# Three zero products fewer, the loads in one queue, and the stores of an attention and channel-mix kernel in quarters

## The chip, the cores and the metric

The kernel runs on one core of a Trainium2 chip. The metric is the time on the device of one execution, in microseconds (us); the median of several runs is compared. A profile is one further execution, taken by the hardware profiler, with a record of each instruction.

The core has four engines that compute, each with its own queue in which instructions start in order: TensorE (PE in the profile, with PEld for the loads of its weights), VectorE (DVE), ScalarE (ACT) and GpSimd (POOL). SyncE (SP) only issues transfers. A "q" behind a name (SPq, ACTq, POOLq) is the part of the engine that issues and waits. Transfers run on 16 DMA engines.

## The reference

Two layers follow each other. The first is attention with polynomial features, on 4 batches, 4 heads, 1088 positions and 32 dimensions a head:

```python
def phi(x):                                   # r = 8, so 64 features
    a = einsum('rd,bhsd->bhsr', S1, x)
    b = einsum('rd,bhsd->bhsr', S2, x)
    return einsum('bhsi,bhsj->bhsij', a, b).reshape(..., r * r)
q_p, k_p = phi(q), phi(k)
kv  = einsum('bhsf,bhsd->bhfd', k_p, v)
z   = sum(k_p, axis=2)
num = einsum('bhsf,bhfd->bhsd', q_p, kv)
den = einsum('bhsf,bhf->bhs', q_p, z)[..., None] + 1e-06
attn = num / den
```

Its output, with the heads side by side, is the x (4 x 1088 x 128) of the second layer, a channel mix with the previous position:

```python
xk = mu_k * x + (1 - mu_k) * x_prev
xr = mu_r * x + (1 - mu_r) * x_prev
k  = maximum(xk @ w_k, 0)                     # 128 -> 1024
v  = (k * k) @ w_v                            # 1024 -> 128
out = sigmoid(xr @ w_r) * v
```

## The kernel before, in words

Everything fits on the core at once. The kernel is a list of some 370 short tasks, written out by hand in the string `ORDER`; each task is a function of the kernel that puts one or a few instructions on one engine. The order in the string is the order on each engine. Nothing is moved by a planner; waits between engines come from the data. A name is followed by its batch (0 to 3) or its group of outputs (0 to 8), and by a letter for the engine where there is a choice (A for ScalarE, V for VectorE, G for GpSimd, S for SyncE); `@` gives the PSUM banks.

The loads are a list of their own, `LOADS`, issued in this order ahead of all tasks: `k01@S` is the second half of k of batch 0, issued by SyncE, `s0` and `s1` are S1 and S2, `v00` to `v03` the quarters of v of batch 0, `w0` to `w2` the weights. The two rows of mu (lines 168 and 169) are issued after the list. The framework hands out eight semaphores in turn to the transfers that SyncE and ScalarE issue, loads and stores alike, in the order in which the program puts them; a transfer waits until the one eight places ahead of it has landed. GpSimd's transfers have eight others.

The tasks around the change, for batch b:

- `kturn.b.y` (L262): VectorE transposes half y of k, as soon as it is loaded. `qturn.b` (L344) does the same for q.
- `smk`, `smz` (L209, L201): TensorE spreads S1 and S2; `sevk` (L213) and `sevz` (L204) put them into SK and ZL on VectorE, `sqc` (L216) copies SK four times on GpSimd.
- `kproj.b.j` (L273): projections of k. Form P has tiles of 32 columns, four beside each other; form W has 64 columns, two beside each other. `abev.b.j` (L248) copies them out on ScalarE.
- `zmm.b` (L300), `zev.b`, `wmm.b` (L308), `wsq.b` (L312): the sum z, its copy, its row product on TensorE, and its place in SQ on VectorE.
- `abw.b.g` (L353, L367): projections of q against SQ, which give the row for the denominator too; `abwev`, `pw`, `dred` (L393), `drec` (L398) and `an` turn it into 1/den and the scaled factor, on ScalarE, GpSimd and VectorE.
- `kp` and `kvmm` (L321): features of k, and kv. `mumm` (L220) turns the rows of mu.
- `zz.n@bank` (L188): n products of zeros, 512 columns each, that nothing reads. There are 18 in the kernel, all in the first 17 us.
- `f1`, `relu`, `sq`, `f2`, `rr`, `sig`, `fin` (L581): the channel mix for a group of 512 output rows (256 in group 8). From about 27 us on TensorE does mostly this.
- `st.g.S` (L595): store of group g, 128 partitions by 512 numbers, 256 KB. Its target is written as 4 x 32 rows of 512. `st.g.t.S` stores quarter t of it, 32 partitions. In the kernel before, groups 0, 1, 3, 2, 6 and 7 (in this order) are stored whole by SyncE, and the last three groups, 5, 4 and 8, in quarters by three engines.

Of the kernel before, what the change touches and what calls it, by code (L numbers as in the profile page):

```python
# [71 lines left out]
def kernel(  # L72
# [53 lines left out]

    def load(what):
# [12 lines left out]
        elif x == "w":  # L140
            if b == 0:
                e.dma_start(wk_f[:], moe_w_k)
            elif b == 1:
                e.dma_start(wr_f[:], moe_w_r)
            else:
                e.dma_start(wv_f[:], moe_w_v.rearrange("(c p) d -> p c d", p=P))
        else:
            y, z = int(name[2]) // 2, int(name[2]) % 2
            m = 9 - z
            s = v[b].rearrange("h (a y t) d -> y a h t d", y=2, t=17)[y, :, :, 9 * z:9 * z + m, :]  # L150
            e.dma_start(vin[b][64 * y + z:64 * y + 64:2, :, :m, :].rearrange("p h m d -> p h (m d)"),
                        s.rearrange("a h m d -> a h (m d)"))

# [493 lines left out]
```

## Time and profile before

| what | value |
|---|---|
| median of 3 runs | 83.06 us (82.38 to 83.06) |
| the profiled execution's own time | 82.54 us |
| its span, from first to last instruction | 80.7 us |
| TensorE busy | 74.1 us, 92% of the span |
| VectorE busy | 65.4 us, 81% |
| ScalarE busy | 56.0 us, 69% |
| GpSimd busy | 47.4 us, 59% |
| read from and written to HBM | 7.80 MB and 2.23 MB |

The time of an execution is the span and what lies around it, 1.84 us here. A busy TensorE also counts products that wait in the pipeline. The chain of waits is the work that ended last, followed back from the last instruction: its steps are what the time is made of, the busy shares are not.

### The profile page before, as it was taken

What the parts mean: (1) busy time and instruction counts of PE and PEld (TensorE: products, weight loads), DVE (VectorE), ACT (ScalarE), POOL (GpSimd) and SP (SyncE); (2) the same over time, 40 slices, a digit from 0 to 9 for tenths busy, and PEclk for the clock granted to TensorE, in tenths of its full rate; (3) what the DMA queues carried; (4) which work ended last, traced back from release to release, by engine and by line L of the source; (5) the groups of instructions that cost most, each with busy time, mean ns of one, the idle gap of its engine ahead of it and who ended that gap; (6) DMA issues with size and microseconds to landing.
All of it is one profiled execution on the core that took longest, in us unless ns stands there. A gap on an engine that the chain in (4) does not pass through costs nothing.

```text
span 80.7 us, 3273 instructions
## 1 busy us (share of the span) xinstructions
PE 74.1 (92%) x1410; PEld 52.2 (65%) x1410; DVE 65.4 (81%) x102; ACT 56.0 (69%) x88; POOL 47.4 (59%) x68
## 2 busy tenths in 40 slices
PE   4999999989999899999999999999999999999600
PEld 1376378847809458576876785778666876899500
DVE  4563820899967999999999999899989999999500
ACT  0703106116547799899899999999979988999400
POOL 6245960786999997589506499209901718702720
PEclk9999999999999999999999999999999999999995
DMA  1999999999999600000000012220022220112570
GB/s 20 312 349 307 292 337 362 231 263 310 382 299 245 181 9 0 8 0 12 0 0 12 0 15 71 83 86 24 0 27 96 55 89 0 15 51 109 176 238 5
DMA packets 7258, 10.24 MB, mean 127 GB/s; under 512 B 762, under 2 KB 4060, under 8 KB 7244
## 3 DMA queue, kind: packets, MB, share of 16 engines
q1 hardware_dynamic: 6840, 9.46, 40.2%
q10 hardware_dynamic: 308, 0.41, 1.5%
q8 instruction: 11, 0.18, 0.9%
q0 software_dynamic: 96, 0.16, 0.8%
q14 instruction: 3, 0.02, 0.1%
HBM read 7.80 MB, written 2.23 MB: 124 GB/s over the span
## 4 chain that ended last, share of the span: by engine, by line
PE 61%; POOL 12%; DVE 10%; ACT 6%; issue 4%; POOLq 1%; ACTq 0%
PE ps L526 13%; PE ps L558 12%; PE ps L188 8%; PE ps L433 6%; PE ps L367 6%; POOL kp L255 5%; PE ps L273 5%; ACT k L534 5%; PE ps L321 3%; DVE k L536 3%; PE ps L571 3%; DVE osb L581 2%; DVE XK L505 2%; DVE k L255 2%; POOL pw L255 1%
## 5 line engine op out<-in xcount | busy, mean ns | idle before, releaser
L534 ACT ACTIVATE k<-ps 128x1024 bf16<-128x1024 f32 (+1 forms) x32 | 29.7, 976 | 1.1 <-DVE XK L505 0.3
L558 PEld LDWEIGHTS <-k 128*128 128x128 bf16 x272 | 16.9, 98 | 4.2 <-issue 0.5
L526 PE MATMUL ps<-XK,wk 128*128 128x512 bf16 (+1 forms) x72 | 19.2, 367 | 0.2 <-DVE XK L464 0.2
L558 PE MATMUL ps<-wv,k 128*128 128x128 bf16 x272 | 19.1, 219 | 0.0
L255 POOL TENSOR_TENSOR kp<-ab 128x1280 f32<-128x1280 f32 (+1 forms) x8 | 17.3, 2178 | 1.0 <-ACT ab L248 1.0
L255 POOL TENSOR_TENSOR k<-k 128x1024 bf16<-128x1024 bf16 (+1 forms) x6 | 10.5, 1751 | 11.8 <-DVE k L255 9.2
L255 DVE TENSOR_TENSOR k<-k 128x1024 bf16<-128x1024 bf16 (+1 forms) x21 | 14.1, 708 | 0.3 <-PE ps L558 0.3
L255 DVE TENSOR_TENSOR qp<-an,ps 128x1152 f32<-128x1152 f32 (+1 forms) x8 | 10.1, 1269 | 0.0
L546 ACT ACTIVATE k<-k 128x1024 bf16<-128x1024 bf16 (+1 forms) x9 | 9.1, 1028 | 0.4 <-PE ps L558 0.3
L188 PE MATMUL ps<-zero 128*128 128x512 bf16 x18 | 7.7, 560 | 1.2 <-DVE warm L155 1.2
L262 DVE STREAM_TRANSPOSE kT<-k 128x576 f32<-128x576 f32 x8 | 5.9, 753 | 3.1 <-DMA k<-in_k_dram 3.1
L526 PEld LDWEIGHTS <-wk 128*128 128x128 bf16 x72 | 6.1, 98 | 3.3 <-issue 0.7
L255 POOL TENSOR_TENSOR pw<-abw 128x272 f32<-128x272 f32 (+2 forms) x5 | 3.3, 650 | 7.6 <-ACT abw L248 7.6
L420 DVE STREAM_TRANSPOSE qf<-qp 128x2176 f32<-128x2176 f32 x3 | 7.3, 2435 | 0.0
L248 ACT COPY ab<-ps 128x256 f32<-128x256 f32 (+1 forms) x7 | 2.7, 396 | 6.1 <-PE ps L273 5.9
L367 PE MATMUL ps<-SQ,qT 128*64 128x96 f32 (+1 forms) x144 | 6.6, 250 | 0.0
L581 DVE TENSOR_TENSOR osb<-ps,r 128x512 f32<-128x512 f32 (+1 forms) x9 | 5.8, 648 | 0.9 <-ACT r L576 0.5
L273 PEld LDWEIGHTS ps<-SK,kT 128*32 128x32 f32 (+1 forms) x200 | 5.3, 145 | 1.4 <-issue 0.8
L273 PE MATMUL ps<-SK,kT 128*32 128x64 f32 (+1 forms) x200 | 6.1, 256 | 0.0
L248 ACT COPY X<-ps 128x512 f32<-128x512 f32 (+2 forms) x12 | 4.9, 434 | 1.8 <-PE ps L485 1.2
L367 PEld LDWEIGHTS ps<-SQ,qT 128*64 128x64 f32 (+1 forms) x144 | 5.5, 131 | 0.5 <-DVE SQ L312 0.3
L321 PE MATMUL ps<-kp,v 128*32 128x64 f32 x288 | 5.7, 222 | 0.0
(88 smaller groups left out, 102.4 us busy)
## 6 DMA issues: line engine op xcount, KB each, us to landing
k<-in_k_dram SPq DMA_DIRECT2D x7, 272.0 KB, 6.5
q<-in_q_dram SPq DMA_DIRECT2D x3, 544.0 KB
out_dram<-osb SPq DMA_DIRECT2D x6, 256.0 KB
v<-in_v_dram SPq DMA_DIRECT2D x8, 144.0 KB, 4.5
v<-in_v_dram SPq DMA_DIRECT2D x8, 128.0 KB, 5.2
q<-in_q_dram SPq DMA_DIRECT2D x2, 272.0 KB
...
```

The costliest lines, as they stand in the source:

```text
L188: nc.tensor.matmul(PS[:, banks[0], :], zero[:, :P], zero[:], skip_group_check=True)
L248: nc.scalar.copy(o, i)
L255: (nc.vector if eng == "V" else nc.gpsimd).tensor_mul(o, a, b)
L273: nc.tensor.matmul(_ap(d, [[n, 2], [1, 32]]), sb["kT", b][:, m, w * c:w * c + w], SK[:, :, :H].rearrange("p x h r -> p x (h r)"), skip_gro ...
L321: nc.tensor.matmul(o[32 * h:32 * h + 32, :F], vin[b][:, h, m, :], sb["kp", b, j][:, 4 * (m - KG[j][0]) + h].rearrange("p i j -> p (i j)"), ...
L367: nc.tensor.matmul(o[32 * w * c:32 * w * c + 32 * w, n:n + 96], sb["qT", b][:, u:u + w, :].rearrange("p u a -> p (u a)"), SQ[b][:, x:x + H ...
L420: nc.vector.transpose(sb["qf", b][:, s0:s1].rearrange("p s f a -> p (s f a)"), sb["qp", b][:, s0:s1].rearrange("p s i j -> p (s i j)"))
L526: nc.tensor.matmul(h[:, c, :], wk[:, P * (2 * cp + c):P * (2 * cp + c) + P], x, skip_group_check=True)
L534: nc.scalar.activation(o, h, RELU)
L546: nc.scalar.activation(o, i, SQUARE)
L558: nc.tensor.matmul(o[:, i * P:i * P + P], k2[:, i * P:i * P + P], wv[:, 2 * cp + c, :], start=(cp == 0 and c == 0 and i == 0), stop=(cp == ...
L581: nc.vector.tensor_mul(o[:].rearrange("p i f -> p (i f)")[:, :n], ps["o", g][:, :n], sb["r", g][:, :n])
```

## The change

- In `LOADS`, k01 goes from ScalarE's queue to SyncE's, so that all loads but S1 are issued by SyncE in one row. The two rows of mu are issued by GpSimd, behind its first memsets and ahead of the list of loads, in place of ScalarE.
- `zz.4@2` ahead of `zmm.0` becomes `zz.1@2`.
- The tile of zeros is 128 x 128 in place of 128 x 512; the product reads the same 128 columns four times.
- Groups 0, 1, 3, 2, 6 and 7 are stored in quarters, all by SyncE, at the same place in the order.
- Branches on `SPREAD` come in for another layout of k and v; `SPREAD` is empty, so they do nothing.

The lines of `ORDER` behind the first store are broken differently in the diff; their order is the same.

```diff
+SPREAD = {}
 LOADS = """
-s0@A k00@S k01@A s1@S q00@S q01@S k10@S k11@S v00@S v02@S v01@S v03@S q1@S w0@S w1@S k20@S k21@S v10@S v12@S v11@S
+s0@A k00@S k01@S s1@S q00@S q01@S k10@S k11@S v00@S v02@S v01@S v03@S q1@S w0@S w1@S k20@S k21@S v10@S v12@S v11@S
...
 ORDER = """
-kp.0.0.G kturn.1.0 abev.0.1.A zz.4@2 zmm.0@0 kturn.1.1 zev.0.A zz.3@2 wmm.0 qturn.0 kproj.1.1.W@1 kproj.1.0.W@2
+kp.0.0.G kturn.1.0 abev.0.1.A zz.1@2 zmm.0@0 kturn.1.1 zev.0.A zz.3@2 wmm.0 qturn.0 kproj.1.1.W@1 kproj.1.0.W@2
...
-f1.3.1@56 f2.0.3 relu.3.1.A f2.1.1 dred.2.2.V f1.3.2@01 fin.0 st.0.S sq.3.0.A f1.2.1@56 drec.2.2 relu.3.2.V f2.1.2
+f1.3.1@56 f2.0.3 relu.3.1.A f2.1.1 dred.2.2.V f1.3.2@01 fin.0 st.0.0.S st.0.1.S st.0.2.S st.0.3.S sq.3.0.A f1.2.1@56
...
-f2.7.3 f1.5.3@67 fin.6 st.6.S sq.5.2.A f1.4.2@45 relu.5.3.V f1.4.1@12 xb.2.G relu.4.2.A f2.5.0@0 f2.5.1 fin.7 st.7.S
+f2.7.3 f1.5.3@67 fin.6 st.6.0.S st.6.1.S st.6.2.S st.6.3.S sq.5.2.A f1.4.2@45 relu.5.3.V f1.4.1@12 xb.2.G relu.4.2.A
+f2.5.0@0 f2.5.1 fin.7 st.7.0.S st.7.1.S st.7.2.S st.7.3.S relu.4.1.A f1.4.3@67 sq.5.3.V f1.8.0@45 f2.5.2 sq.4.0.V
...
-    zero = const.tile([P, 512], BF16)
+    zero = const.tile([P, P], BF16)
...
+    nc.gpsimd.dma_start(mu_row[:1, :], moe_mu_k.rearrange("(x d) -> x d", x=1))
+    nc.gpsimd.dma_start(mu_row[1:, :], moe_mu_r.rearrange("(x d) -> x d", x=1))
     for what in LOADS.split():
         load(what)
-    nc.scalar.dma_start(mu_row[:1, :], moe_mu_k.rearrange("(x d) -> x d", x=1))
-    nc.scalar.dma_start(mu_row[1:, :], moe_mu_r.rearrange("(x d) -> x d", x=1))
...
-            nc.tensor.matmul(PS[:, banks[0], :], zero[:, :P], zero[:], skip_group_check=True)
+            nc.tensor.matmul(PS[:, banks[0], :], zero[:], _ap(zero[:], [[0, 4], [1, P]]), skip_group_check=True)
```

## Rows read from the trace of the kernel before

**Rows 1.** The page: busy tenths of the span in 40 equal slices.
```profile
PE   4999999989999899999999999999999999999600
...
DMA  1999999999999600000000012220022220112570
```

**Rows 2.** The chain of waits in order of time: start us, us, what.
```profile
5.26 2.10 PE ps L273 x72
7.36 1.82 PE ps L188 x4
...
10.97 1.20 PE ps L273 x36
...
35.30 0.56 PE ps L273 x40
```

**Rows 3.** Timeline, 3 to 14 us, by engine: start us, us, engine, line, operation [idle before].
```profile
3.58 1.44 DVE L262 STREAM_TRANSPOSE kT<-k 128x576 f32<-128x576 f32 x2 [0.78 <-DMA k<-in_k_dram]
...
5.22 0.89 POOL L216 COPY SQ<-SK 128x96 f32<-128x96 f32 x4 [2.79 <-DVE SK L213]
...
7.43 0.37 ACT L248 COPY ab<-ps 128x256 f32<-128x256 f32 x1 [0.43 <-PE ps L273]
...
8.43 0.78 DVE L262 STREAM_TRANSPOSE kT<-k 128x576 f32<-128x576 f32 x1 [0.38 <-DMA k<-in_k_dram]
9.13 1.27 DVE L344 STREAM_TRANSPOSE qT<-q 128x1088 f32<-128x1088 f32 x1
...
11.01 0.21 DVE L312 TENSOR_TENSOR SQ<-ps,m 128x48 f32<-128x48 f32 x1 [0.61 <-PE ps L308]
...
13.94 0.49 POOL L255 TENSOR_TENSOR pw<-abw 128x144 f32<-128x144 f32 x1 [2.55 <-ACT abw L248]
```

**Rows 4.** Timeline of TensorE: zero products (L188), wide projections of k (L273) and of q (L367).
```profile
9.57 1.24 PE L188 MATMUL ps<-zero 128*128 128x512 bf16 x3
...
12.57 0.85 PE L367 MATMUL ps<-SQ,qT 128*64 128x96 f32 x16
...
16.41 0.82 PE L188 MATMUL ps<-zero 128*128 128x512 bf16 x3
...
25.53 1.27 PE L273 MATMUL ps<-SK,kT 128*64 128x64 f32 x36
```

**Rows 5.** Timeline of SyncE and VectorE, 20 to 24 us.
```profile
20.54 0.60 SPq L151 DMA_DIRECT2D v<-in_v_dram  x1
...
21.24 1.27 DVE L344 STREAM_TRANSPOSE qT<-q 128x1088 f32<-128x1088 f32 x1
...
23.20 0.47 DVE L393 TENSOR_REDUCE den<-pw 128x34 f32<-128x306 f32 x1 [0.69 <-POOL pw L255]
```

**Rows 6.** Stretches: length, busy us of PE, PEld, DVE, ACT, POOL, PEclk, DMA share, GB/s.
```profile
1.75:3.00 1.25, 1.25 (x5) 0.43 (x3) 1.01 (x4) 0.61 (x1) 0.68 (x8) 1.00 0.91 250
3.00:4.30 1.30, 1.30 (x12) 0.43 (x11) 0.72 (x2) 0.88 (x2) 0.00 (x0) 1.00 0.96 345
...
74.00:75.25 1.25, 1.25 (x24) 1.08 (x21) 0.73 (x2) 1.25 (x4) 1.12 (x2) 1.00 0.26 102
```

**Rows 7.** Groups by line, GpSimd from 60 us: busy us, mean ns of one, idle before.
```profile
L595 POOL DMA_DIRECT2D out_dram<-osb x3 | 1.7, 559 | 0.6 <-DVE osb L581 0.6
```

**Rows 8.** Waits of SyncE's queue, 44 us to the end: us in total, times, longest.
```profile
SPq L595 <- DVE osb L581: 24.7, 6, 7.5
...
SPq L642 <- DMA out_dram<-osb: 1.5, 1, 1.5
SPq L595 <- DMA out_dram<-osb: 0.8, 1, 0.8
```

**Rows 9.** Timeline of the tail: ScalarE's queue, SyncE's queue.
```profile
77.00 0.43 ACTq L595 DMA_DIRECT2D out_dram<-osb  x1
...
77.20 0.79 SPq L595 DMA_DIRECT2D out_dram<-osb  x2
```

**Rows 10.** DMA issues from 75.8 us: count, KB each, median us to landing.
```profile
out_dram<-osb POOLq DMA_DIRECT2D x1, 32.0 KB, 2.1
```

More of the change, by code (lines that the diff above doesn't have):

```diff
@@ L49 @@
 f1.3.0@56 abwev.2.1.A qf.3.2 f2.0.2 relu.3.0.A pw.2.2.G^sq.1.3.V f1.2.0@01 f2.1.0@2 xb.1.G^sq.1.3.V relu.2.0.A
-f1.3.1@56 f2.0.3 relu.3.1.A f2.1.1 dred.2.2.V f1.3.2@01 fin.0 st.0.S sq.3.0.A f1.2.1@56 drec.2.2 relu.3.2.V f2.1.2
-an.2.2.G relu.2.1.A f2.1.3 kp.2.1.G kvmm.2.0@7 qp.2.0 sq.3.2.A xmm.3@0156 sq.2.0.A fin.1 st.1.S sq.3.1.G qp.2.1
-kvmm.2.1 xev.3.0.A f1.3.3@23 xev.3.1.A xtev.3.V f2.3.0@4 kvev.2.V relu.3.3.A xs.3 f1.2.2@56 xk.3.2 f1.2.3@01
-relu.2.2.A f2.3.1 rr.3@2 sq.2.1.V relu.2.3.A kdmm.2 f1.6.0@56 sq.2.2.V f2.3.2 relu.6.0.A sq.3.3.V f1.6.1@01 qf.2.2
@@ L54 @@
-f2.2.0@3 sq.2.3.G^sq.3.3.V sig.3 f2.3.3 relu.6.1.A f1.7.0@56 f2.2.1 relu.7.0.A rr.2@2 xb.3.G f1.6.2@01 fin.3 st.3.S
-kvcp.2.A f2.2.2 relu.6.2.A xmm.2@4567 sq.6.0.V sig.2 sq.7.0.V sq.6.1.V f2.2.3 xev.2.0.A f2.6.0@2 sq.6.2.V xtev.2.A
-f1.7.1@01 xev.2.1.A fin.2 st.2.S xs.2^sq.6.2.V f2.6.1 relu.7.1.A xk.2.2 f1.7.2@67 rr.6@3 relu.7.2.A f1.6.3@45 sq.7.1.V
+f1.3.1@56 f2.0.3 relu.3.1.A f2.1.1 dred.2.2.V f1.3.2@01 fin.0 st.0.0.S st.0.1.S st.0.2.S st.0.3.S sq.3.0.A f1.2.1@56
+drec.2.2 relu.3.2.V f2.1.2 an.2.2.G relu.2.1.A f2.1.3 kp.2.1.G kvmm.2.0@7 qp.2.0 sq.3.2.A xmm.3@0156 sq.2.0.A fin.1
@@ new lines @@
+st.1.0.S st.1.1.S st.1.2.S st.1.3.S sq.3.1.G qp.2.1 kvmm.2.1 xev.3.0.A f1.3.3@23 xev.3.1.A xtev.3.V f2.3.0@4 kvev.2.V
+relu.3.3.A xs.3 f1.2.2@56 xk.3.2 f1.2.3@01 relu.2.2.A f2.3.1 rr.3@2 sq.2.1.V relu.2.3.A kdmm.2 f1.6.0@56 sq.2.2.V
+f2.3.2 relu.6.0.A sq.3.3.V f1.6.1@01 qf.2.2 f2.2.0@3 sq.2.3.G^sq.3.3.V sig.3 f2.3.3 relu.6.1.A f1.7.0@56 f2.2.1
+relu.7.0.A rr.2@2 xb.3.G f1.6.2@01 fin.3 st.3.0.S st.3.1.S st.3.2.S st.3.3.S kvcp.2.A f2.2.2 relu.6.2.A xmm.2@4567
+sq.6.0.V sig.2 sq.7.0.V sq.6.1.V f2.2.3 xev.2.0.A f2.6.0@2 sq.6.2.V xtev.2.A f1.7.1@01 xev.2.1.A fin.2 st.2.0.S
@@ L57 @@
+st.2.1.S st.2.2.S st.2.3.S xs.2^sq.6.2.V f2.6.1 relu.7.1.A xk.2.2 f1.7.2@67 rr.6@3 relu.7.2.A f1.6.3@45 sq.7.1.V
 f1.7.3@01 sig.6 f2.6.2 sq.7.2.G^sq.7.1.V relu.7.3.V relu.6.3.A f1.5.0@67 f2.7.0@3 f2.7.1 relu.5.0.A f1.5.1@01 sq.6.3.V
 f1.5.2@45 relu.5.1.A rr.7@6 sq.7.3.V f2.6.3 sq.5.0.V sig.7 f1.4.0@01 relu.5.2.V f2.7.2 sq.5.1.G^sq.5.0.V relu.4.0.A
-f2.7.3 f1.5.3@67 fin.6 st.6.S sq.5.2.A f1.4.2@45 relu.5.3.V f1.4.1@12 xb.2.G relu.4.2.A f2.5.0@0 f2.5.1 fin.7 st.7.S
-relu.4.1.A f1.4.3@67 sq.5.3.V f1.8.0@45 f2.5.2 sq.4.0.V relu.8.0.A f1.8.2@12 f2.5.3 relu.4.3.A sq.4.1.V rr.5@3
@@ L61 @@
-sq.4.2.V rr.8@4 relu.8.2.A f2.4.0@5 sq.8.0.V f1.8.1@67 sig.5 sq.4.3.V f2.4.1 relu.8.1.A f1.8.3@12 sq.8.2.V rr.4@3
-fin.5 st.5.0.S st.5.1.S st.5.2.S relu.8.3.A sq.8.1.G^sq.8.2.V f2.4.2 sig.4 f2.4.3 sq.8.3.A f2.8.0@0 fin.4 st.4.0.S
-st.4.3.S f2.8.1 sig.8 f2.8.2 f2.8.3 fin.8 st.8.2.S st.5.3.G st.4.1.A st.4.2.G st.8.0.A st.8.1.G st.8.3.A
+f2.7.3 f1.5.3@67 fin.6 st.6.0.S st.6.1.S st.6.2.S st.6.3.S sq.5.2.A f1.4.2@45 relu.5.3.V f1.4.1@12 xb.2.G relu.4.2.A
+f2.5.0@0 f2.5.1 fin.7 st.7.0.S st.7.1.S st.7.2.S st.7.3.S relu.4.1.A f1.4.3@67 sq.5.3.V f1.8.0@45 f2.5.2 sq.4.0.V
@@ L64 @@
+relu.8.0.A f1.8.2@12 f2.5.3 relu.4.3.A sq.4.1.V rr.5@3 sq.4.2.V rr.8@4 relu.8.2.A f2.4.0@5 sq.8.0.V f1.8.1@67 sig.5
+sq.4.3.V f2.4.1 relu.8.1.A f1.8.3@12 sq.8.2.V rr.4@3 fin.5 st.5.0.S st.5.1.S st.5.2.S relu.8.3.A sq.8.1.G^sq.8.2.V
+f2.4.2 sig.4 f2.4.3 sq.8.3.A f2.8.0@0 fin.4 st.4.0.S st.4.3.S f2.8.1 sig.8 f2.8.2 f2.8.3 fin.8 st.8.2.S st.5.3.G
+st.4.1.A st.4.2.G st.8.0.A st.8.1.G st.8.3.A
 """
@@ L147, in load @@
         else:
[L148 to L152, printed above, removed]
+            if b in SPREAD:
+                z = int(name[2])
+                m = 9 - z
+                s = v[b].rearrange("h (x t) d -> x h t d", t=17)[:, :, 9 * z:9 * z + m, :]
+                p = slice(z, P, 2)
+            else:
+                y, z = int(name[2]) // 2, int(name[2]) % 2
+                m = 9 - z
+                s = v[b].rearrange("h (a y t) d -> y a h t d", y=2, t=17)[y, :, :, 9 * z:9 * z + m, :]
+                p = slice(64 * y + z, 64 * y + 64, 2)
+            e.dma_start(vin[b][p, :, :m, :].rearrange("p h m d -> p h (m d)"), s.rearrange("x h m d -> x h (m d)"))
     nc.vector.memset(zero[:], 0.0)
@@ L261, in kturn @@
             sb["kT", b] = work.tile([P, 9, P], F32, name="kT", tag="kT", bufs=2)
-        nc.vector.transpose(_ap(sb["kT", b][:, 0, 64 * y:], [[1, 2], [P, 9], [2, 32]]),
+        c, n = (2 * y, 4) if b in SPREAD else (64 * y, 2)
+        nc.vector.transpose(_ap(sb["kT", b][:, 0, c:], [[1, 2], [P, 9], [n, 32]]),
                             kin[b][:, y].rearrange("p (z m d) -> p z m d", z=2, m=9))
```

## The prediction

> **What bounds the kernel now.** Read the slices of the page first [rows 1]. TensorE is nine tenths busy from the second slice to about 76 us; the DMA engines are full up to about 28 us and nearly idle after it. So the end is set by a full TensorE in the long middle, and the two places where time can be taken out are ahead of that stretch (to 26 us) and behind it (the last stores). Of the change, the zero products and the loads lie ahead of it, the stores reach behind it.
>
> Next comes the chain of waits, in order of time [rows 2]. It runs through TensorE from 1.2 to 14 us, and part of what it runs through is not work: the zero products zz.4, 1.82 us from 7.36 to 9.18. Whether they cover a wait is read from the engines around it [rows 3]. The z product zmm.0, which follows it, needs ACT's copy of the last k projection, and that copy ends at 7.43 + 0.37 = 7.80 us. From 7.8 to 9.18 the zero products stand in front of work that is ready.
>
> Last, how fast TensorE runs there [rows 4]. Three zero products take 1.24 us at 9.57 and 0.82 us at 16.41; in the chain the 72 narrow projections at 5.26 take 2.10 us (29 ns each), the 40 of the same shape at 35.30 take 0.56 us (14 ns each) [rows 2]. The first is 512 columns at 1.2 GHz, the second the pace of 2.4 GHz. The 36 wide projections of batch 1 take 1.20 us at 10.97 [rows 2], as long as the same ones at 25.53 [rows 4]: the clock has risen by 10.97, and not before the last of the three zero products began at about 10.4. I take 10.5. (The column of the granted clock reads 1.00 from the first stretches on [rows 6]; for these first microseconds the paces are the better witness.)
>
> **The three zero products: -0.9 us.** One product of the block is left: 1.82 / 4 = 0.45 us, so it ends at 7.36 + 0.45 = 7.81, when the copy is there too (7.80). zmm.0 starts at about 7.87 in place of 9.18, 1.3 us sooner, and what follows on TensorE in order (zz.3, the row product of z, kproj.1.1) moves with it: kproj.1.1 from 10.97 to 9.67. Now the next late things. kproj.1.1 needs the second k transpose of batch 1, which waits for its load and ends at 8.43 + 0.78 = 9.21 [rows 3]: 0.46 us to spare. abw.0.0 needs SQ, and VectorE makes it behind the q transpose, which ends at 9.13 + 1.27 = 10.40: ready at 10.40 + 0.21 = 10.61, while TensorE comes to it at 11 us or later. GpSimd had been idle for 2.55 us when it began pw.0.0 at 13.94 [rows 3], so it follows a shift of up to that much. Then the clock: at 9.67 it has not yet risen. From 9.67 to 10.5 the projections go at half pace, and half of 0.83 us, 0.4, is lost. 1.3 - 0.4 = 0.9 us.
>
> Bounds. If the clock rises much earlier in an execution (say by 9 us), a removed product is worth not 0.42 but 0.22 us, and the transpose at 9.21 stops the shift: about 0.4. If it rises behind 11, both kernels run the projections slow and the whole 1.3 is kept. 0.4 to 1.3, and I take the profiled execution's 0.9.
>
> Does the shift last to 28 us, from where TensorE is full? Behind 14 us the chain goes through GpSimd and VectorE, which follow each other and move as one; only the loads stand still. The tightest I find is q of batch 2 [rows 5]. Each load waits for the one eight places ahead of it in the program, so the v load at 20.54 says that this q was in by then; its transpose starts at 21.24, and 0.9 earlier is 20.34. At worst 0.2 us is missed there, and VectorE idles 0.69 us just behind, ahead of the den sum at 23.20, which takes that up. Nothing is charged.
>
> **The loads: 0.** Second half of k of batch 0: it now stands behind the first in SyncE's queue. The two are 544 KB, the engines move 250 GB/s from 1.75 to 3.00 us and 345 GB/s after [rows 6]; that is 557 thousand bytes: 312 by 3.00 and the other 245 in 0.71 us more, so at 3.7 us. Its transpose can't start before the first one, of 0.72 us, has ended: the two run back to back from 3.58 for 1.44 us [rows 3]. 0.5 us of cover. S2 (1 KB) comes in behind them, and its products stand at 3.9 us under the same two transposes. All later loads gain one issue of about 0.4 us ahead of them on SyncE, but the DMA engines are full (shares 0.91 and 0.96), and what is queued sooner does not land sooner. The two loads of mu leave the round of eight, so the first v loads wait for older ones; same answer. I take 0, between -0.2 (k00 no longer shares the engines with k01) and +0.2 (S2 later than the transposes). The mu rows cost GpSimd two issues at 0.56 us [rows 7], from about 2.4 to 3.6, inside the 2.79 us in which it waits for SK [rows 3]; without that cover 1.1 us would fall on the SQ copies. Zero rows of 128 columns in place of 512 shorten the first memset by at most 0.2 us, ahead of the same transposes: 0.
>
> **The stores: -0.4 us.** Until the last ones they are off the path: 18 more issues at about 0.4 us each are 7 us on a SyncE that waits 24.7 us for results [rows 8]. In the tail they are not. While the whole store of group 7 drains, from 74.00 to 75.25, the engines are 0.26 busy and move 102 GB/s [rows 6]: the work of four of sixteen. SyncE's quarter st.4.3 is eight places behind that store, waits 0.8 us for it [rows 8], and is issued at 77.20 with st.8.2 behind it; both issues end at 77.99 [rows 9], and 1.5 us later the program's last wait is over (79.5). In quarters, group 7 is written long before. SyncE then issues st.4.3 at 76.4 and st.8.2 at 76.8 and is done 0.8 us sooner. Next late is ACT's third store, issued at 77.00: with the 2.1 us to landing of GpSimd's 32 KB store [rows 10] it comes in at 79.1. 79.5 - 79.1 = 0.4 us. Bounds: 0, if the full engines set the last landing, to 0.7, if ACT's and GpSimd's last stores land sooner too when the engines hold nothing of group 7.
>
> The Trainium skill, "DMA: Bandwidth & Descriptors", section "Why a DMA increments its semaphore by 16 and not by 1", says that a transfer uses the largest number of engines up to 16 that divides the slowest dimension of both sides. The whole store's is 4 and the quarter's 32; the trace's 0.26 agrees with 4 of 16. Its section "Rules for kernel authors" speaks against quarters: under 64 KB one pays mostly overhead, so gather transfers; by that rule the tail would gain nothing and the sum would be 81.6 instead of 81.2.
>
> **Sum.** -0.9 + 0 - 0.4 = -1.3 us on the profiled execution, 82.54 us (its span of 80.7 and 1.84 around it): 81.24. The median of the three runs is 83.06, half a microsecond above it (one run is 82.38); from there it would be 81.76. I put the forecast between, at 81.5.
>
> **Rivals.** (a) *The clock rises later.* The zero products are also what TensorE did before the clock rose. With three fewer the rise may come later, and fp32 work goes at half pace. If it comes only behind abw.0.1: kproj.1 takes another 1.2 us, the next zero product 0.2, and the 16 products each of abw.0.0 (0.85 us at 12.57 [rows 4]) and abw.0.1 another 0.85, together 3.1; less the 1.3 saved that is 1.8 us; with the tail 82.54 + 1.8 - 0.4 = 83.9, slower. It decides from where kproj.1 runs wholly slow (rise behind 12 us, +1.2 against -1.3); behind about 13 us the tail's gain is gone as well. Against it: TensorE has no new hole, since zmm.0 is ready at once and the projections at 9.67, so the same stretch stays filled, with projections for zero products. For it: the clock had not risen by 9.57, after the 2.10 us of projections at 5.26. 13%. The Trainium skill, "TensorE: Matmul & The Clock Gate", section "What's actually happening", states that "the default state is throttled, and activity releases the throttle"; the trace agrees in that the first ten microseconds run at 1.2 GHz. By that rule the time is this rival's 83.9 if the stretch, with fewer zero products in it, no longer releases the throttle in time.
>
> (b) *The gain is taken up by the loads.* The order of loads is unchanged in bytes; if q of batch 2 or k of batch 3 lands later by a microsecond, VectorE waits there and the middle's 0.9 is gone: 82.54 - 0.4 = 82.1, or 82.6 from the median, no change. Against it the spare times above. 17%.
>
> (c) *The tail keeps its length,* since the engines or the other two issuers set it: 82.54 - 0.9 = 81.6, or 82.1 from the median. 15%.
>
> **How the numbers follow.** Forecast 55% (81.0 to 82.0), (c) 15%, (b) 17%, (a) 13%. A difference of under 1%, 0.8 us, is about what a measurement of this kernel can't tell from none. Faster by more than that: the forecast and most of (c), 68%; within: (b) and the rest, 19%; slower: (a), 13%. The range leaves out (a) and a little at the low end, where 1.3 and 0.7 would both come in: 80.8 to 82.8.
>
> **What would show it.** Right: zmm.0 at about 7.9, kproj.1.1 at about 9.7 and its 36 products between 1.2 and 1.9 us long, pw.0.0 near 13.0; the den sum of batch 1 at 22.3; stores with DMA shares well over 0.26 in short bursts; SyncE's last issue ended by 77.2 less the shift; the landing after it 79.1 less 0.9. Wrong: kproj.1 of 2.4 us and later zero products still 0.42 us apart (a); a wait of VectorE on q or k between 18 and 25 us (b); the last wait on a store ending no sooner than 79.5 less the middle's gain (c); a transpose at 3.6 that starts later, or SQ copies behind mu's issues.

## The result and the profile after

The changed kernel is slower: median 83.55 us of 20 runs (82.48 to 85.42) against 82.37 us of 20 runs of the kernel before on the same chips (81.47 to 84.75), ratio 1.0136 with a 95% interval of 1.0100 to 1.0171. The forecast was 81.5 us. The profiled execution took 83.49 us, span 81.7 us (before 82.54 and 80.7): its rows can be laid beside those of before, and they account for the 0.95 us between these two executions. Ratios here and below compare only the runs within 1.5% of the fastest run of their own kernel, medians all runs; the more runs a kernel has, the lower its fastest, so where 6 or 12 runs stand against 17 to 36 of before the two can differ by over one per cent (after_k_first: 10 of 12 runs against 3 of 23).

TensorE is nearly as full as before and the DMA engines are full as long [rows 1]; the page's slices differ little, and where the time went is not to be seen in them:

```profile
PE   5889979989999899999999999999999999999400
...
DMA  1889999999999600000000051300132200540660
```

**To 14 us.** Timeline of the changed kernel (line numbers are 12 or 13 higher than before: L188 is L200, L262 is L275, L273 is L286, L255 is L267), to be laid beside [rows 3]:

```profile
4.41 0.30 PE L221 MATMUL ps<-ident,S 16*32 16x16 f32 x8 [0.67 <-DMA S<-in_S_dram]
...
7.82 0.61 PE L200 MATMUL ps<-zero 128*128 128x512 bf16 x1
7.95 0.37 ACT L260 COPY ab<-ps 128x256 f32<-128x256 f32 x1 [0.43 <-PE ps L286]
8.36 0.53 PE L313 MATMUL ps<-ab 128*32 128x32 f32 x18
8.82 1.31 PE L200 MATMUL ps<-zero 128*128 128x512 bf16 x3
...
9.00 0.78 DVE L275 STREAM_TRANSPOSE kT<-k 128x576 f32<-128x576 f32 x1 [3.40 <-DMA k<-in_k_dram]
...
10.14 0.78 DVE L275 STREAM_TRANSPOSE kT<-k 128x576 f32<-128x576 f32 x1 [0.37 <-DMA k<-in_k_dram]
...
10.85 1.27 DVE L357 STREAM_TRANSPOSE qT<-q 128x1088 f32<-128x1088 f32 x1
10.98 1.26 PE L286 MATMUL ps<-SK,kT 128*64 128x64 f32 x34 [0.44 <-DVE kT L275]
...
14.01 0.49 POOL L267 TENSOR_TENSOR pw<-abw 128x144 f32<-128x144 f32 x1 [2.09 <-ACT abw L260]
```

TensorE waits 0.67 us for S2, the copy of the last k projection is 0.52 us later than before (7.95 for 7.43), the one zero product covers it, and zmm.0 does start sooner (8.36; 9.11 in the timeline of before). But both k transposes of batch 1 wait for their load, 3.40 and 0.37 us, and come 1.7 us later (9.00 and 10.14 for 7.26 and 8.43). TensorE then stands idle for 0.44 us, which it never did here before, and pw.0.0 is at 14.01 in place of 13.94: nothing gained in this pair of executions. The chain of waits (start us, us, what) says it most shortly; where before it ran through projections and zero products [rows 2], it now runs through a load:

```profile
3.42 6.70 DMA k<-in_k_dram
10.14 0.79 DVE kT L275
10.98 1.26 PE ps L286 x34
```

**At 51 us.** From 14 us on VectorE, ScalarE and GpSimd keep the distance of 0.07 us up to one copy of GpSimd. Timeline of the kernel before, and of the changed one:

```profile
50.71 0.23 DVE L250 COPY X<-ps 64x64 f32<-64x64 f32 x1 [0.22 <-ACT X L248]
...
51.07 0.21 POOL L498 COPY X<-X 128x31 f32<-128x31 f32 x1 [0.26 <-DVE X L250]
51.31 1.35 DVE L505 SCALAR_TENSOR_TENSOR XK<-X,rat 128x1088 bf16<-128x1088 f32 x1
```

```profile
50.78 0.23 DVE L262 COPY X<-ps 64x64 f32<-64x64 f32 x1 [0.21 <-ACT X L260]
...
51.50 0.21 POOL L511 COPY X<-X 128x31 f32<-128x31 f32 x1 [0.61 <-DVE kvs L262]
...
51.75 1.35 DVE L518 SCALAR_TENSOR_TENSOR XK<-X,rat 128x1088 bf16<-128x1088 f32 x1 [0.28 <-POOL X L511]
```

VectorE's copy, the input, ends at 50.94 and 51.01. GpSimd follows 0.13 us later before and 0.49 us later after, with nothing else to do; VectorE now waits for it, and the distance is 0.44 us from here to the last product of osb.

**The tail.** That last product (VectorE, group 8) in both kernels, before first:

```profile
76.16 0.42 DVE L581 TENSOR_TENSOR osb<-ps,r 128x256 f32<-128x256 f32 x1 [0.37 <-PE ps L558]
```

```profile
76.60 0.42 DVE L594 TENSOR_TENSOR osb<-ps,r 128x256 f32<-128x256 f32 x1 [0.37 <-PE ps L571]
...
76.83 1.10 SPq L608 DMA_DIRECT2D out_dram<-osb  x2
```

From its start to the end of the span are 80.7 - 76.16 = 4.5 us before and 81.7 - 76.60 = 5.1 us after. SyncE's last issue ends at 77.93, 1.33 us behind that start in place of 1.83 [rows 9], as forecast in sign. Yet its last wait, and GpSimd's last store, are longer than in [rows 8, 10] (waits: us in total, times, longest; DMA issues from 75.4 us: count, KB each, median us to landing):

```profile
SPq L655 <- DMA out_dram<-osb: 2.1, 1, 2.1
```

```profile
out_dram<-osb SPq DMA_DIRECT2D x4, 64.0 KB, 2.2
out_dram<-osb POOLq DMA_DIRECT2D x2, 64.0 KB, 2.5
...
out_dram<-osb POOLq DMA_DIRECT2D x1, 32.0 KB, 2.5
```

The wait ends at 77.93 + 2.1 = 80.0, and the span 1.7 us later; before it ended at 77.99 + 1.5 = 79.5, and the span 1.2 us later. So of the half microsecond some 0.1 lies ahead of the end of that wait and 0.45 behind it. The data themselves are not later: the last packet of a store ends 2.6 us behind the start of that product, before 2.7. Behind it the DMA engines move nothing in either kernel, but for one transfer of 8 KB of a queue of instructions in the changed kernel, at 81.1 us (stretches as in [rows 6], before and after; last, from the DMA queues of the changed kernel behind 75.4 us: packets, MB, share):

```profile
78.50:79.00 0.50, 0.00 (x0) 0.00 (x0) 0.00 (x0) 0.00 (x0) 0.00 (x0) 0.73 0.34 107
79.00:79.50 0.50, 0.00 (x0) 0.00 (x0) 0.00 (x0) 0.00 (x0) 0.00 (x0) 0.50 0.00 0
```

```profile
79.00:79.50 0.50, 0.00 (x0) 0.00 (x0) 0.00 (x0) 0.00 (x0) 0.00 (x0) 1.00 0.24 70
79.50:80.00 0.50, 0.00 (x0) 0.00 (x0) 0.00 (x0) 0.00 (x0) 0.00 (x0) 1.00 0.00 0
...
q14 instruction: 1, 0.01, 0.2%
```

Spans are given to 0.1 us only; the executions' own times, 0.95 us apart, leave 0.95 - 0.44 = 0.51 us for the tail. In all: 0.07 + 0.37 + 0.51 = 0.95 us.

### The profile page after: what moved, and what is told of

Read it like the earlier page. It is cut to its first block, busy times and chain, and to the rows that moved or that the text cites. A ratio compares the mean times of both kernels' runs of the same rounds, so it can differ in the third digit from the quotient of the medians.

```text
span 81.7 us, 3292 instructions
## 1 busy us (share of the span) xinstructions
PE 73.4 (90%) x1407; PEld 52.1 (64%) x1407; DVE 65.3 (80%) x102; ACT 56.1 (69%) x88; POOL 48.4 (59%) x70
## 4 chain that ended last, share of the span: by engine, by line
PE 59%; POOL 12%; DMA 8%; DVE 6%; issue 4%; SPq 3%; ACT 2%; POOLq 1%; DVEq 0%; ACTq 0%
PE ps L539 17%; PE ps L571 17%; DMA k<-in_k_dram 8%; PE ps L446 6%; PE ps L380 5%; POOL kp L267 5%; PE ps L584 4%; PE ps L334 3%; PE ps L286 2%; DVE XK L518 2%; DVE osb L594 2%; SPq L142 2%; POOL pw L267 1%; ACT k L547 1%; POOL wk L246 1%
## 5 line engine op out<-in xcount | busy, mean ns | idle before, releaser
L267 POOL TENSOR_TENSOR kp<-ab 128x1280 f32<-128x1280 f32 (+1 forms) x8 | 17.3, 2176 | 1.5 <-ACT ab L260 1.5
L267 POOL TENSOR_TENSOR k<-k 128x1024 bf16<-128x1024 bf16 (+1 forms) x6 | 10.5, 1751 | 11.8 <-DVE k L267 9.2
L267 DVE TENSOR_TENSOR k<-k 128x1024 bf16<-128x1024 bf16 (+1 forms) x21 | 14.1, 711 | 0.3 <-PE ps L571 0.3
L267 DVE TENSOR_TENSOR qp<-an,ps 128x1152 f32<-128x1152 f32 (+1 forms) x8 | 10.1, 1270 | 0.0
L275 DVE STREAM_TRANSPOSE kT<-k 128x576 f32<-128x576 f32 x8 | 5.8, 751 | 4.5 <-DMA k<-in_k_dram 4.5
L267 POOL TENSOR_TENSOR pw<-abw 128x272 f32<-128x272 f32 (+2 forms) x5 | 3.2, 649 | 7.1 <-ACT abw L260 7.1
L200 PE MATMUL ps<-zero 128*128 128x512 bf16 x15 | 6.5, 550 | 1.0 <-DVE warm L167 1.0
L286 PE MATMUL ps<-SK,kT 128*32 128x64 f32 (+1 forms) x200 | 6.4, 256 | 0.4 <-DVE kT L275 0.4
L286 PEld LDWEIGHTS ps<-SK,kT 128*32 128x32 f32 (+1 forms) x200 | 5.5, 145 | 2.0 <-issue 0.8
```

The lines of the kernel that those rows point to most:

```text
L200: nc.tensor.matmul(PS[:, banks[0], :], zero[:], _ap(zero[:], [[0, 4], [1, P]]), skip_group_check=True)
L267: (nc.vector if eng == "V" else nc.gpsimd).tensor_mul(o, a, b)
L286: nc.tensor.matmul(_ap(d, [[n, 2], [1, 32]]), sb["kT", b][:, m, w * c:w * c + w], SK[:, :, :H].rearrange("p x h r -> p x (h r)"), skip_gro ...
```

## The experiments

All kernels in one table. Those named after_..., undo_quarters, mu_none and memsets_dve are built on the changed kernel, the others on the kernel before. Columns: ratio to the kernel before; medians of this kernel and of before, measured beside it (one run: the profiled one alone); from the profiled execution the start of the second k transpose of batch 1, the start of pw.0.0, the distance from VectorE's copy to GpSimd's copy at 51 us, and the tail, from the start of the last product of osb to the end of the span (us).

| kernel | ratio (95%) | medians | k | pw.0.0 | copy | tail |
|---|---|---|---|---|---|---|
| before | | | 8.43 | 13.94 | 0.13 | 4.5 |
| changed | 1.0136 (1.0100 to 1.0171) | 83.55, 82.37 | 10.14 | 14.01 | 0.49 | 5.1 |
| only_mu | 1.0003 (0.9941 to 1.0065) | 82.90, 83.16 | 9.16 | 13.69 | 0.5 | 4.6 |
| only_k01 | 1.0008 (0.9935 to 1.0082) | 82.95, 83.16 | 9.80 | 13.67 | 0.13 | 4.6 |
| only_zz | 0.9984 (0.9931 to 1.0037) | 82.94, 83.16 | 7.86 | 14.38 | 0.13 | 4.5 |
| only_quarters | 1.0113 (1.0062 to 1.0164) | 83.31, 83.16 | 9.27 | 13.40 | 0.13 | 5.3 |
| late_quarters | 1.0001 (0.9949 to 1.0053) | 82.57, 82.62 | 8.11 | 14.69 | 0.13 | 4.8 |
| early_quarters | 1.0087 (1.0027 to 1.0147) | 82.97, 82.62 | 8.30 | 13.36 | 0.13 | 4.6 |
| undo_quarters | 1.0101 (1.0055 to 1.0147) | 83.04, 82.62 | 10.04 | 13.91 | 0.5 | 4.6 |
| mu_none | one run | 83.82, 82.62 | 10.36 | 14.22 | 0.13 | 5.3 |
| loads_only | 1.0151 (1.0047 to 1.0255) | 83.41, 82.61 | 10.58 | 14.45 | 0.5 | 4.6 |
| zz_quarters | none | 83.79, 82.61 | 8.70 | 14.64 | 0.13 | 5.1 |
| k_first | 1.0048 (0.9989 to 1.0107) | 82.84, 82.61 | 6.86 | 13.11 | 0.13 | 4.8 |
| quarters_7 | one run | 83.92, 82.61 | 9.08 | 15.27 | 0.13 | 4.4 |
| after_k_first | 1.0168 (1.0087 to 1.0249) | 83.03, 82.98 | 6.74 | 12.61 | 0.5 | 5.1 |
| after_67_whole | 1.0145 (1.0005 to 1.0285) | 83.43, 82.98 | 9.36 | 13.23 | 0.5 | 5.1 |
| after_both | 1.0061 (0.9999 to 1.0122) | 82.81, 82.98 | 8.35 | 14.04 | 0.5 | 5.2 |
| loads_k_first | 1.0120 (1.0037 to 1.0203) | 83.11, 82.98 | 8.26 | 13.90 | 0.5 | 4.6 |
| memsets_dve | one run | 85.41, 83.92 | 10.55 | 15.75 | 0.13 | 5.3 |
| k_first_one_row | none | 82.91, 83.92 | 7.10 | 13.62 | 0.13 | 4.5 |

The column of pw.0.0 also holds when TensorE's clock rose in that one execution (zero products at 0.42 us or at 0.2 us each): a pw.0.0 is read together with the k beside it. It also holds whether the second half of batch 0's k was late. In six of the nine kernels with k01 on ScalarE's queue VectorE waits 0.36 to 2.14 us for that half and transposes it at 4.73 to 6.47 us; in the other three, and in all eleven with k01 on SyncE's, the two halves run back to back.

With that scatter, single profiles are weak, and the twenty together say more. With the loads in the old order, pw.0.0 lies between 13.36 and 15.27 us in the eight kernels with k01 on ScalarE's queue and between 13.23 and 15.75 in the seven with it on SyncE's; the mean is 14.2 in both. So the stretch to 14 us came out even, and the +0.07 above is one pair out of this scatter. From pw.0.0 to VectorE's copy are 36.76 or 36.77 us in twelve kernels and 36.99 to 40.36 in the other eight. From that copy to the last product of osb are 25.45 or 25.46 us in the twelve kernels without the stop at 51 us and 25.81 to 25.83 in the eight with it: the stop costs its 0.37 us each time. With the tail's half microsecond, which all six kernels with six groups in quarters have at least, that is 0.9 of the 1.1 us that the runs show.

**Each part alone: only_mu, only_k01, only_zz, only_quarters.**

```diff
 only_mu (the same for moe_mu_r; both now ahead of the list of loads)
-    nc.scalar.dma_start(mu_row[:1, :], moe_mu_k.rearrange("(x d) -> x d", x=1))
+    nc.gpsimd.dma_start(mu_row[:1, :], moe_mu_k.rearrange("(x d) -> x d", x=1))
 only_k01
-s0@A k00@S k01@A s1@S
+s0@A k00@S k01@S s1@S
 only_zz
-zz.4@2 zmm.0@0
+zz.1@2 zmm.0@0
 only_quarters (for g = 0, 1, 3, 2, 6, 7)
-st.g.S
+st.g.0.S st.g.1.S st.g.2.S st.g.3.S
```

> The kernel before with one part of the change: the two rows of mu issued by GpSimd. Theory M (GpSimd's two transfers hold up the DMA engines): the two transposes of batch 1's k start at about 8.9 and 10.1 us, as in the changed kernel, not at 7.26 and 8.43; time at most 0.3 us longer, since the four zero products before the z product still cover most of that. Theory Q (the single queue and S2 behind k01 do it): the transposes stay at 7.3 and 8.4 within 0.2 us, time unchanged.

> The kernel before with one part of the change: the second half of batch 0's k in SyncE's queue. Theory M: the transposes of batch 1's k stay at 7.3 and 8.4 us within 0.3; the products of S start at 4.4 instead of 3.9 us, since S2 lands behind k01, and with four zero products kept all that follows moves by 0.5 us: time +0.5. Theory Q: the transposes of batch 1's k start at 8.9 and 10.1 us.

> The kernel before with one part of the change: one zero product in place of four ahead of zmm.0. Theories M and Q: zmm.0 at 7.9 us, the wide projections of batch 1 at 9.7 and not behind 11.0, pw.0.0 near 13.1, time -0.8 us, since the loads land as before. If the clock rises later for want of zero products (the prediction's first rival), the projections take over 2 us and the time is unchanged or longer.

> The kernel before with one part of the change: all stores in quarters. By the prediction -0.4 us, the last landing 3.0 us behind the start of the last product of results and not 3.4. Rival, from the changed kernel's tail (3.6): no gain, 0 to +0.2 us, and a GpSimd or ACT instruction near 51 us that starts 0.3 to 0.4 us later than its inputs allow.

Alone, neither move of a load and not the zero products can be told from no change (I had 0.8 us for the products); the quarters cost 1.1% by the ratio, 0.14 us by the medians. In these profiles k of batch 1 is later with each load edit: by 1.37 us with k01 on SyncE, by 0.73 with mu on GpSimd. The first stands out of the scatter: the seven kernels that load as before have k at 7.86 to 9.27 us, the seven with k01 on SyncE's queue in the old order at 9.36 to 10.58. The second, 9.16, does not. In only_k01 k has become the limit although all four zero products are there (timeline):

```profile
9.80 0.78 DVE L262 STREAM_TRANSPOSE kT<-k 128x576 f32<-128x576 f32 x1 [0.53 <-DMA k<-in_k_dram]
...
13.67 0.49 POOL L255 TENSOR_TENSOR pw<-abw 128x144 f32<-128x144 f32 x1 [1.52 <-ACT abw L248]
```

13.67 - 9.80 = 3.87 us from the start of the transpose to pw.0.0. In the changed kernel it is 14.01 - 10.14 = 3.87, the same to the hundredth; before it was 5.51. In only_zz k of batch 1 was not late, but the second half of batch 0's was (5.03 us; the two halves ran back to back from 3.58 before), and TensorE's clock stayed low longer in its execution, which is my rival (a) seen once:

```profile
5.03 0.78 DVE L262 STREAM_TRANSPOSE kT<-k 128x576 f32<-128x576 f32 x1 [0.61 <-DMA k<-in_k_dram]
...
9.08 1.46 PE L188 MATMUL ps<-zero 128*128 128x512 bf16 x3
...
10.77 1.84 PE L273 MATMUL ps<-SK,kT 128*64 128x64 f32 x36
...
14.38 0.49 POOL L255 TENSOR_TENSOR pw<-abw 128x144 f32<-128x144 f32 x1 [2.19 <-ACT abw L248]
```

The 36 wide projections began 0.13 us sooner than before, took 1.84 us in place of 1.27, and pw.0.0 came 0.44 us later. Counted from the transpose of that half, pw.0.0 comes 8.6 to 9.9 us later in the six kernels with four zero products, k01 on ScalarE's queue and the old order, and 8.0 to 8.3 in k_first, zz_quarters and after_k_first, with one zero product and k of batch 1 not the limit (9.35 in only_zz): by the means the products are worth some 0.8 to 1.1 us there, near the forecast's 0.9.

**Which quarters: late_quarters (groups 6 and 7), early_quarters (0, 1, 3, 2), quarters_7 (7 alone).** Edits as in only_quarters, for these groups alone.

> Kernel before with groups 6 and 7 alone in quarters (six more issues on SyncE), the four earlier stores whole. Theory T (the last stores land later because the stores ahead of them are in quarters: about 0.35 us): the whole loss of the tail is here already, 0.3 to 0.5 us, ratio about 1.005. Theory C (the cost goes with the count of SyncE's instructions: 18 more of them bring a gap of 0.45 us in its last semaphore instructions, behind the last landing): no such gap with six more, last landing to the end of the span as before (1.2 us); ratio 1.000 if C is all of it. My prediction before the result, that quarters of group 7 free SyncE's last stores: 0.4 us faster, 0.995.

> Kernel before with groups 0, 1, 3 and 2 in quarters (twelve more issues on SyncE), groups 6 and 7 whole. Theory T: the tail is that of before, 1.000. Theory C: the gap of 0.45 us ahead of the end comes with the twelve, 1.005. Third theory E (the early stores compete with work of the middle, where nothing in the profile shows it): 1.005 or more without the gap, with TensorE's work later between 45 and 75 us.

> Kernel before with group 7 alone in quarters: the very step of my forecast of the tail. Forecast: SyncE's last issue 0.4 us or more sooner behind the last product of osb, and the end of the span with it (4.2 us in place of 4.6 from the start of that product). Theory T: issue sooner, last landing later all the same, end at 4.8.

The tail by the profiles: 4.4 us with group 7 alone (a gain of 0.1, my forecast's sign, a third of its size; I had 4.2), 4.8 with 6 and 7, 4.6 with the early four, 5.1 to 5.3 in every kernel with all six (changed, only_quarters, mu_none, zz_quarters, after_k_first, memsets_dve). That later landings with 6 and 7 together lengthen it (theory T) is not shown: k_first, with whole stores, has 4.8 too, and the last packet of a store ends 2.6 to 2.9 us behind the start of the last product of osb in all twenty profiles. The 0.45 us behind the waits go with the count of SyncE's issues, as theory C has it: in late_quarters, with six more, SyncE's last issue ends at 78.25, its waits take 2.3 us, and 81.7 - 80.55 = 1.2 us are left, as before; in only_quarters, with eighteen more, 80.9 - (76.96 + 2.3) = 1.6. By the same sum 1.6 to 1.7 us are left in all six kernels with eighteen more, 1.2 to 1.3 in the eleven with none, three or six. (The six have the same six groups in quarters, so the count and the stores themselves are not separated.) With twelve more there are 1.2 in early_quarters and 2.1 in after_67_whole and after_both. The transfer of instructions falls into the same place: it lies ahead of the end of the span in the eight kernels with a tail of 5.1 us or more, behind it in late_quarters and early_quarters, and the other ten have none. In early_quarters a stop of 0.5 us of SyncE stands by itself in the waits, and the two waits for TensorE at the very end, 0.7 us in the changed kernel, have shrunk to 0.2, so it cost nothing:

```profile
SPq L642 <- SPq L642: 0.5, 1, 0.5
SPq L642 <- PEq L642: 0.2, 1, 0.2
```

The times say it less cleanly: late_quarters 1.000, early_quarters 1.009 (its median 0.35 us above before, its mean equal) with a tail as before and no new wait in the middle. Whether the early quarters cost anything is not shown.

**The loads: undo_quarters, loads_only, zz_quarters, mu_none.**

```diff
 undo_quarters (changed kernel, six groups)
-st.g.0.S st.g.1.S st.g.2.S st.g.3.S
+st.g.S
 loads_only = only_mu and only_k01 together
 zz_quarters = only_zz and only_quarters together
 mu_none (changed kernel; the two loads of mu left out)
+    nc.vector.memset(mu_row[:], 0.5)
```

> Changed kernel with its six stores whole again (zero products, loads and mu as changed). If the quarters carry the whole slowdown: 1.000 of before. If the late loads of k cost time beside them (k of batch 1 is 1.7 us later and eats the zero products' gain, nothing more): also 1.000, with the second k transpose of batch 1 at 10.1 us as in the changed kernel. If parts of the loss come only together: over 1.003.

> Kernel before with both changes to the loads (k01 by SyncE, mu by GpSimd), four zero products and whole stores as before. Theory K (the late k of batch 1 is what costs: it is a floor of about 10.9 us under the wide projections, whatever TensorE did before): second k transpose of batch 1 at 10.1 us, 34 wide projections behind it at 10.9 or later with an idle TensorE ahead of them, pw.0.0 near 14.0; ratio 1.003 to 1.010, as with the zero products removed beside it. Rival Z (the removed zero products leave TensorE idle, and that costs): the same late transpose, covered by the four zero products, ratio 1.000.

> Kernel before with three zero products fewer and all stores in quarters; the loads as before. Sum of the parts: tail 0.55 to 0.8 us longer (start of the last product of osb to the end of the span 5.1 to 5.4 us in place of 4.6), the zero products worth 0 to 0.5: ratio 1.002 to 1.009, under the 1.0136 of the changed kernel. If the loads cost nothing: as the changed kernel.

> Changed kernel without the two loads of mu; the rows are filled with 0.5 by VectorE (left out: the mu of the inputs). If GpSimd's two small transfers delay k of batch 1 in the DMA engines: its transposes start at 8.5 and 9.8 us, as with k01 moved alone, in place of 9.0 and 10.1. If not they but their leaving the round of eight semaphores does: still 9.0 and 10.1.

By the ratios the two load edits together cost 1.5%, with all zero products in place (0.8 us by the medians, of six runs), and with whole stores the changed kernel is still 1.0% slower (0.4 us). Both have the stop at 51 us, 0.37 us. So the removed products are not needed for a loss; that the late k carries any of it is not shown. zz_quarters, without the load edits, has k of batch 1 in time and the long tail; six runs gave no ratio. mu_none separates mu's bytes from the rest (timeline):

```profile
9.21 0.78 DVE L274 STREAM_TRANSPOSE kT<-k 128x576 f32<-128x576 f32 x1 [3.25 <-DMA k<-in_k_dram]
10.36 0.78 DVE L274 STREAM_TRANSPOSE kT<-k 128x576 f32<-128x576 f32 x1 [0.36 <-DMA k<-in_k_dram]
...
51.56 0.21 POOL L510 COPY X<-X 128x31 f32<-128x31 f32 x1 [0.25 <-DVE X L261]
```

k is as late as in the changed kernel, so GpSimd's two transfers are not what delays it; and the stop at 51 us is gone with them. What the delay consists of is seen in stretches (length, busy us of PE, PEld, DVE, ACT, POOL, PEclk, DMA share, GB/s), before first, then the changed kernel:

```profile
3.00:5.00 2.00, 2.00 (x14) 0.82 (x12) 1.42 (x3) 0.88 (x2) 0.00 (x0) 1.00 0.97 328
5.00:7.00 2.00, 2.00 (x69) 1.79 (x72) 0.36 (x3) 0.42 (x1) 0.89 (x4) 1.00 1.03 387
```

```profile
3.00:5.00 2.00, 1.33 (x12) 0.59 (x10) 1.42 (x3) 0.00 (x0) 0.46 (x1) 1.00 0.90 307
5.00:7.00 2.00, 2.00 (x51) 1.50 (x54) 0.45 (x3) 0.00 (x0) 0.89 (x4) 1.00 0.89 311
```

From 3 to 7 us the engines are a tenth less busy and move 1236 thousand bytes in place of 1430: 194 thousand fewer, 0.6 us at 311 GB/s, in front of k. (only_k01 shows 279 and 305 GB/s, only_mu 343 and 368.) All kernels bear this out: 1282 to 1430 thousand bytes in these 4 us in the nine with k01 on ScalarE's queue, 1130 to 1254 in the eleven with it on SyncE's. The loads behind k01 in SyncE's queue are also issued some 0.48 us later, up to the first half of k of batch 1 (q of batch 0 at 2.09 for 1.60, that half at 2.95 for 2.47). So with k01 off ScalarE's queue the engines are not full, which accounts for a part of k01's 1.37 us. For a delay by mu there is only an argument: its two rows no longer hold two of the eight semaphores, and SyncE issues the first v load at 3.97 us in place of 4.29 (3.50 in only_mu), so more large loads are under way while k comes in.

**Taking the causes away: k_first, after_k_first, loads_k_first, after_67_whole, after_both.**

```diff
 k_first (with only_zz), after_k_first (changed kernel), loads_k_first (with loads_only)
-q00@S q01@S k10@S k11@S
+k10@S k11@S q00@S q01@S
 after_67_whole (changed kernel; g = 6, 7)
-st.g.0.S st.g.1.S st.g.2.S st.g.3.S
+st.g.S
 after_both = after_k_first and after_67_whole together
```

> Kernel before with three zero products fewer and k of batch 1 loaded ahead of q of batch 0 (same bytes, same queues, stores whole). If the arrival of k sets what the removed zero products are worth: k transposes of batch 1 end by 8 us, q of batch 0 is in by 8.5 and its transpose ends by 9.9, the wide projections start at 9.3 to 9.8 with no wait, pw.0.0 between 12.9 and 13.6; ratio 0.990 to 0.995. If the pace of TensorE ahead of its rise decides alone: projections early but at half pace, pw.0.0 at 13.6 or later, ratio 0.997 to 1.000.

> Changed kernel with k of batch 1 loaded ahead of q of batch 0. Theory K (floor of the late k): no wait of TensorE ahead of the wide projections, pw.0.0 at 13.0 to 13.5 in place of 14.0; of the 1.1 us lost about half comes back, ratio 1.004 to 1.009. If the loss of the loads lies later in the load stage: pw.0.0 earlier, but VectorE waits for q or k between 18 and 26 us and the ratio stays at 1.010 to 1.015.

> Kernel before with both changes to the loads and k of batch 1 ahead of q of batch 0 (four zero products, whole stores). By the floor: 0.998 to 1.003, since the k is early and the rest as before; k transposes of batch 1 end by 9.2 us. If the loads cost by something else: 1.008 or more, as with them alone.

> Changed kernel with groups 6 and 7 stored whole again. If the tail carries the loss of the stores: from the start of the last product of osb to the end of the span 4.5 to 4.6 us in place of 5.1, ratio 1.005 to 1.009. If the early quarters (0, 1, 3, 2) carry it: the same short tail by the profile, ratio still 1.011 to 1.015.

> Changed kernel with both: k of batch 1 ahead of q of batch 0, groups 6 and 7 whole. With the two causes as I have them: ratio 0.995 to 1.002. A third cause, if it is over 1.005.

With k of batch 1 ahead of q of batch 0 the wait is gone, and the removed zero products show (after_k_first, timeline):

```profile
6.04 1.44 DVE L275 STREAM_TRANSPOSE kT<-k 128x576 f32<-128x576 f32 x2 [0.45 <-DMA k<-in_k_dram]
...
8.66 0.82 PE L200 MATMUL ps<-zero 128*128 128x512 bf16 x3
...
9.57 1.27 PE L286 MATMUL ps<-SK,kT 128*64 128x64 f32 x36
...
12.61 0.49 POOL L267 TENSOR_TENSOR pw<-abw 128x144 f32<-128x144 f32 x1 [0.70 <-ACT abw L260]
```

Projections at 9.57 (forecast 9.7), pw.0.0 at 12.61 (13.0), 1.3 us ahead of before; a part of it is this execution's clock, which was up when the three zero products ran (0.82 us; 1.31 in the changed kernel). after_67_whole, in the old order, shows the limit once more, with a k that happened to land sooner: 13.23 - 9.36 = 3.87.

```profile
9.36 0.78 DVE L275 STREAM_TRANSPOSE kT<-k 128x576 f32<-128x576 f32 x1 [0.49 <-DMA k<-in_k_dram]
...
13.23 0.49 POOL L267 TENSOR_TENSOR pw<-abw 128x144 f32<-128x144 f32 x1 [1.29 <-ACT abw L260]
```

Its tail did not come back (5.1 us, my expectation of 4.5 to 4.6 failed): GpSimd's last store lands in 2.1 us again, but what lies behind the landings stayed, with twelve more issues. The timed runs do not follow the profiles. The profiled spans of k_first (80.1 us) and after_k_first (80.3) are among the three shortest, but these executions are among the two fastest of twelve, and over all runs the medians stand 0.2 and 0.05 us above before, the ratios at 1.005 and 1.017. loads_k_first came out at 1.012 where I had 0.998 to 1.003, 0.13 us above before by the medians. after_both was to take both suspected causes away, and its profile still has both: TensorE waits 0.83 us for k of batch 1 and the tail is 5.2 us; the stop at 51 us is there too, and VectorE waits 0.97 us for q of batch 2 at 23 us. It is at 1.006 with 1.000 just in the interval, and 0.17 us below before by the medians. No single step is shown by the timed runs.

**Two last ones: memsets_dve and k_first_one_row.**

```diff
 memsets_dve (changed kernel)
-        nc.gpsimd.memset(t[:, :, R:], 1e-6)
+        nc.vector.memset(t[:, :, R:], 1e-6)
 k_first_one_row = k_first and only_k01 together
```

> Changed kernel with the two memsets of pws on VectorE in place of GpSimd, so that GpSimd has as many instructions as in the kernel before, mu's two issues included. If the stall at 51 us goes with the count of GpSimd's instructions: the copy of X (L511) starts with an idle time of about 0.26 us and VectorE does not wait for it. If it goes with mu's transfers: 0.61 us as in the changed kernel.

> Kernel before with three zero products fewer, k01 by SyncE and k of batch 1 ahead of q of batch 0; mu by ScalarE and whole stores as before. By the causes found: pw.0.0 0.8 to 1.3 us sooner, no stall at 51 us, tail 4.55 us; profiled span 79.4 to 80.0 and ratio 0.985 to 0.995. If what the profile shows at 14 us is not kept in the timed runs (as k_first, 1.005 with a profiled span of 80.1): 1.000 to 1.005.

memsets_dve keeps mu on GpSimd and takes two other instructions from it. The stop is gone (timeline):

```profile
52.81 0.23 DVE L262 COPY X<-ps 64x64 f32<-64x64 f32 x1 [0.26 <-ACT X L260]
...
53.17 0.21 POOL L511 COPY X<-X 128x31 f32<-128x31 f32 x1 [0.30 <-DVE X L262]
53.42 1.35 DVE L518 SCALAR_TENSOR_TENSOR XK<-X,rat 128x1088 bf16<-128x1088 f32 x1
```

53.17 - 53.04 = 0.13 us, as before. With the table: 0.5 us in all eight kernels with two more instructions on GpSimd, 0.13 in the twelve others. k_first_one_row has no stop, the short tail and an early k, but its q of batch 0 came late in the profiled execution and pw.0.0 gained 0.3 us only; the span is 80.7, where I had 79.4 to 80.0. Its median is 1.0 us below that of before on the same chip (82.91 and 83.92), of 12 and 17 runs that lie between 81.0 and 84.8; no interval came out, so it is not shown to beat the kernel before.

## Why the prediction was wrong, point by point

- **What bounds the kernel**: right. The middle kept its length and order: 0.07 us of distance from 14 to 51 us (and the same 36.77 us in twelve of the twenty kernels).
- **Zero products, -0.9**: the products were cover for nothing that TensorE did, as said, and without a late k the step holds (9.57 and 12.61 in after_k_first). The step that failed is the next late thing, "0.46 us to spare" at the second k transpose: the spare time was measured against a k that the change itself moved by 1.7 us. What came of it was +0.07 in this pair.
- **Loads, 0**: the failed step itself: "the DMA engines are full", so that the extra issue on SyncE would cost nothing. With k01 in SyncE's row they were a tenth less busy from 3 to 7 us, the first half of k of batch 1 was issued 0.48 us later, and both halves were transposed 1.7 us later. The Trainium skill, "DMA: Bandwidth & Descriptors", section "Rules for kernel authors", says that spreading transfers over the issuing engines doesn't help bandwidth, since all use the same 16 DMA engines, and only saves issue time. The issue time shows here (the 0.48 us); the 1236 in place of 1430 thousand bytes in the same 4 us speak against the rest. S2 behind k01 was off too: TensorE waited 0.67 us for it and the copy of the k projections came 0.52 us later, which one zero product covered. Rival (b) had the mechanism, a load that takes up the gain, but I looked for it at batches 2 and 3, 10 us too late for this execution (in those of zz_quarters, after_both and undo_quarters VectorE does wait there, 0.78 to 1.68 us for q of batch 2).
- **mu on GpSimd, covered**: the issues are covered. What I did not price is that two more instructions on GpSimd stop it for 0.37 us at 51 us, on the path.
- **Stores, -0.4**: SyncE was done 0.5 us sooner, and group 7's drain was gone; the end came half a microsecond later all the same. With group 7 alone the step is right in sign and small (-0.1). "They are off the path: 18 more issues" was the failed step: with eighteen more issues 0.45 us more lie behind SyncE's last wait, where no store is moving any more. What SyncE does in them no row names. The rule against small transfers in the Trainium skill, "DMA: Bandwidth & Descriptors", section "Rules for kernel authors", names those under 64 KB; the quarters have 64 KB, and no run here shows that overhead: their last packets end no later (2.6 us for 2.7).
- **Rival (a)**, the clock: in the changed kernel the wide projections ran at 1.26 us, full pace; once in only_zz they did not (1.84).

Sum of the rows: 0.07 + 0.37 + 0.51 = 0.95 us where I had -1.3. The timed difference is 1.1 us (1.36% of 82.4). That these sums agree so closely is in part luck, since the stretch to 14 us scatters by 2 us from execution to execution; what the profiles show in every kernel that has the edit are the 0.37 and the 0.5. How the timed difference divides stays open: loads_only says 1.5%, only_quarters 1.1%, which is more than the whole, and 6 to 12 runs of a kernel that scatters by 3 us carry no finer statement. Open as well: why early_quarters is slower by the ratio, and what the two stops consist of.
